# When weight slabs are requested in the last pass of an attention backward kernel, and which buffers the last ones use

## The chip, the cores and the metric

The kernel runs on one core of one Trainium2 chip. The metric is the time of one execution in device microseconds (us), the median of several runs. A profile is one further execution, recorded instruction by instruction. Engines are named as in the profile: PE (TensorE matmul) and PEld (its weight loads), DVE (VectorE), ACT (ScalarE), POOL (GpSimd), SP (SyncE). SP issues all loads of this kernel, POOL all its stores.

## The reference, cut to what matters

Two blocks alternate, twice each: an attention block for one token (1024 wide, 32 query heads, 4 groups of keys and values of 65,536 positions by 128) and a feed-forward block (3584 wide, squared ReLU). Both uses of a block share their weights and the K and V caches. The kernel returns the output and the gradients of everything for a given grad_out.

```
x = x + A(layernorm(x), K, V, wq, wo)
x = x + B(layernorm(x), w1, b1, w2, b2)
x = x + A(layernorm(x), K, V, wq, wo)
x = x + B(layernorm(x), w1, b1, w2, b2)
out, vjp = jax.vjp(f, x, K, V, wq, wo, w1, b1, w2, b2);  grads = vjp(grad_out)
```

The gradients of K and V are as large as the caches: 64 MB each in bf16 are read in every pass and, in the last one, written too.

## The kernel before, in words

The kernel goes over K and V four times: two forward passes (layers L1 and L3), a backward pass for L3 (`attn_bwd3`), and a last pass (`attn_bwd4`) that does the backward of L1 and writes the gradients of K and V for both layers. Between the passes stand dense stages for the feed-forward blocks. The change touches the last pass, which begins some 1,190 us into the execution.

**Items.** The last pass has 256 items, 64 for each of the 4 groups, in the order of groups 3, 2, 1, 0. An item is 8 columns of 128 positions. `pipeline` (line 828) counts iterations `i` (kept in `NOW["i"]`); a stage with lag n works on an item n iterations after its start. V is read up to 16 items ahead of the rest. Stages that matter here: `vT` (line 1316) turns V on PE (line 1324); `dV8` and `dK8` multiply out gradient blocks (`outer16`, PE line 1396), copy them from PSUM to the arena with ACT or DVE (`evac`, lines 161 and 164) and store them from POOL (line 1402); `k8` (line 1415) multiplies K blocks into the gradient of q (8 matmuls an item, line 1427). A K or V block of 1 MB serves 4 items. The forward passes and `attn_bwd3` run in an order written out by hand (`manual_schedule`); the last pass has none: there the instructions of each engine are put in order by a scheduler, with the program order as priority.

**Slots.** One SBUF tile, the arena, is cut into 20 slots of 1 MB (12 plus 8 that hold softmax numerators, given back as groups end). `take_one` (line 284) hands out a slot in program order, `give_slot` (line 319) takes it back. In the last pass the slots are split in two: a ring for stores (`RING`, 5 slots, and 2 more with each finished group), from which `fill=True` takes the oldest, and the other slots for loads, from which `fill=False` takes the oldest. A slot that was given back after a store counts as free 5 steps later (`STORE_STEPS`). The load itself can go out as soon as the slot's last user is done on the chip.

**Slabs.** `slabs` (line 433) yields a weight matrix row block by row block: in the last pass a slab is 4 row blocks, 1 MB, in one slot, requested by `fetch` at line 450. With `ahead=1` the next slab is requested only when the one before is used up.

**Row dots.** `g_rowdots` (line 565) multiplies 8 row blocks (two slabs) with a vector that is broadcast to all partitions (`g_bcast_vec`, line 547: a PE transpose, a small copy, 8 matmuls at line 558, two ACT copies to `vbc` at line 560). Each row block is one DVE product (line 586) and one ACT sum (line 575). It is a generator that `Background.step` (line 774) advances once an item; a yielded "wait" lets other background work go on in that item. In the last pass six of these jobs run, alternating wo (`g_dO`, for the next group) and wq (`g_dn`, for the group just ended): from iterations 32, 88, 119, 152, 183 and 218. Background work also holds `g_outer_wide` (line 1518), which keeps one load slot for long, and `g_outer`.

**The end.** 20 iterations before the end, two slabs of wq for the last group are requested (line 1845), 10 before the end `fill4` (line 1837) makes a `Rows` with two slots for turned parts (line 609) and fills them; `on4` (line 1818) finishes with the last group.

Of the kernel before, what the change touches and what calls it, by code (L numbers as in the profile page):

```python
# [20 lines left out]
def kernel(  # L21
# [31 lines left out]
    R = HQ // G  # L53
    F = B_w1.shape[1]
    DC, FC = D // P, F // P
# [10 lines left out]
    TLEAD = 2  # L66
    STORE_STEPS = 5
    WAIT_STEPS = 5
    NSLOT = 12
    NWT = 6  # L70
    NKEEP = [8, 7, 7]
# [10 lines left out]
    PS = {}  # L82
# [57 lines left out]
    load = {"act": 0.0, "dve": 0.0, "pe": 0.0}  # L140
# [289 lines left out]
    def f_rows_of(W):  # L430
        return W.rearrange("(s p j) n -> p s j n", p=P, j=4)

    def slabs(name, load, nk, kper, ncols, ahead=1, flat=False):
        pend = deque()
        ks = deque(range(0, nk, kper))

        def fetch():
            k = ks.popleft()
            i = None
            if ks and flat and NOW["wide"] and not odd_one():  # L440
                i = take_pair()
            if i is None:
                kn = min(kper, nk - k)
                sl = Slot(name)
            else:
                kn = min(2 * kper, nk - k)
                ks.popleft()
                sl = Slot(name, at=i, both=True)
            v = sl.t[:, 0:kn * ncols].rearrange("p (k n) -> p k n", n=ncols)
            nc.sync.dma_start(out=v, in_=load(k, kn))  # L450
            pend.append((k, kn, sl, v))

        def gen():
            while ks or pend:
                while ks and len(pend) < ahead:
                    fetch()
                k, kn, sl, v = pend.popleft()
                for kk in range(kn):
                    NOW["slab"] = sl
                    yield k + kk, v[:, kk, :]  # L460
                sl.over = True
                if not sl.users:
                    sl.free()
        g = gen()
        g_fetch = [fetch for _ in range(ahead)]
        return g, g_fetch
# [5 lines left out]
            f()  # L472
        return g

    def wq_slabs(g, ahead=1):
        v = rows_of(A_wq)
        return slabs("s_wq", lambda k, kn: v[:, k:k + kn, g * 1024:(g + 1) * 1024], DC, 4, 1024, ahead, True)

    def wo_slabs(g, ahead=1):
        v = rows_of(A_wo)  # L480
# [2 lines left out]
    def wo_runs(g):  # L483

        v = A_wo[g * 1024:(g + 1) * 1024, :].rearrange("(p k) n -> p k n", k=8)
        return slabs("s_wo", lambda k, kn: v[:, k:k + kn, :], R, 4, 1024, 1, True)[0]

    def w1_slabs(ahead=1):
        v = rows_of(B_w1)
# [72 lines left out]
            yield  # L562
        return vbc

    def g_rowdots(slab_it, nk, vcol, nj, finish, name):
        n = nj * P
        y = vec.tile([P, nk], F32, name=name)
        nc.gpsimd.memset(y[:], 0.0)
        vbc = None
        due = None  # L570
        steps = 8 if PS["pass4"] else WAIT_STEPS

        def total(t, kc):
            def f():
                nc.scalar.activation(out=t[:, :], in_=t[:, :], func=ACTF.Copy, accum_out=y[:, kc:kc + 1])  # L575
            return f
        for kc, slab in slab_it:
            if vbc is None:
                vbc = yield from g_bcast_vec(vcol, nj)
                for _ in range(steps - WAIT_STEPS + 1):  # L580
                    yield "wait"
            elif kc % 4 == 0:
                for _ in range(steps):
                    yield "wait"
            t = mvs.tile([P, n], BF, name="mv_t", tag="mv_t", bufs=2)
            nc.vector.tensor_tensor(out=t[:, :], in0=slab, in1=vbc[:, :], op=ALU.mult)  # L586
            add_load(dve=0.1 + n * 0.00054, act=0.42 + n * 0.00083)
            if due is not None:
                due()
            due = total(t, kc)  # L590
            yield
        due()
        yield
        r = finish(y[:, :])
        if r is not None:
            yield from r
        yield


    class Rows:  # L600
        def __init__(self, pool=None, bufs=NWT):
            self.pool, self.bufs = pool, bufs
            self.views = deque()
            self.n = 0
            self.parts = 0
            if pool is None:

                for _ in range(2):
                    t = Slot("s_wt").t[:, :].rearrange("p (v a b) -> p v a b", v=4, a=8)
                    self.views.extend(t[:, v, :, :] for v in range(4))  # L610
                self.bufs = 8
            self.queue = deque()
            self.jobs = deque()
            self.feed = None
# [282 lines left out]
    def gsl(g):  # L897
        return slice(g * R, (g + 1) * R)
# [10 lines left out]
    def g_wo(L, xacc, g, ps=ps_bg, it=None):  # L909
# [18 lines left out]
        orunb = tmp.tile([P, 8], BF, name="run_ob")  # L928
        nc.vector.tensor_copy(out=orunb[:], in_=oruns[:])
        yield  # L930
        yield from g_mv(wo_runs(g), R, 8, lambda kc: orunb[:, kc:kc + 1], ps, fin)


    def dO_finish(L, g):
# [43 lines left out]
        return fin  # L978

    def g_dn(L, dn, g, first):  # L980
        yield from g_rowdots(wq_slabs(g)[0], DC, L["dqT"][:, gsl(g)], R, dn_finish(dn, first), "%s_dn%d" % (L["name"], g))


    ACT_KT = (3, 13, 15)
# [607 lines left out]
    def pre_load(key, pair):  # L1592
        def f():
            PRE[key] = prefetch(pair())
        return f
# [241 lines left out]
    def fill4():  # L1837
# [4 lines left out]
        PRE["gwq"] = g_outer_last(bgpool, out_4, [L3["n"], L1["n"]], [L3["dqT"][:, gsl(lastg[3])], L1["dqT"][:, gsl(lastg[3])]],  # L1842
                                  lastg[3] * 1024)
        next(PRE["gwq"])
    attn_bwd4(3, L1, L3, on4, bg, b4, [(12 + B4_LAG, last_v), (20, pre_load("wq4", lambda: wq_slabs(lastg[3], 2))), (10, fill4)])
    b4.close()
    ps4_stack.close()

# [29 lines left out]
```

## Time and profile before

| what | value |
|---|---|
| median of 3 runs | 1952.98 us (1948.67 to 1953.23) |
| the profiled execution's own time | 1956.67 us |
| its span, first to last instruction | 1954.7 us |
| busy share of the span: PE, DVE, ACT, POOL | 82%, 60%, 53%, 7% |
| bytes moved | 787.64 MB, mean 403 GB/s |
| issue to landing, median: K and V blocks of 1 MB, slabs of wq in the last pass, stores of 1 MB | 15.6 and 13.1, 22.9, 16.5 us |

The page cuts the span into 40 slices of 48.9 us; a digit is a busy share in tenths, "DMA" the mean busy share of the 16 DMA engines, "GB/s" what they moved. A window view gives the same for any stretch. A waits view names who stood idle for whom: microseconds in total, how many times, and the longest. "issue" as a releaser means that the profile shows nothing that the engine waited for; a line of the engine's sequencer (DVEq) then shows the semaphore instruction that held it. Semaphore and DMA-issuing instructions do not count as busy. The median of K, V and store landings is that of the last pass.

### The profile page before, as it was taken

Reading aid. Unit: us, or ns where it says so; the run is one execution under the profiler, and the core shown is the slowest. Engines: PE = TensorE matmul, PEld = TensorE weight load, DVE = VectorE, ACT = ScalarE, POOL = GpSimd, SP = SyncE. Lnnn points to the kernel's source line nnn. Section 1 sums busy time; section 2 is a strip of 40 time slices with the busy share of each in tenths; the row PEclk is TensorE's granted clock in tenths of the full one; section 3 lists DMA queues with packets and bytes.
Section 4 is the critical chain, followed back from the end, with each engine's and each line's share of the span. In section 5 each row is a group of like instructions: output and inputs, shape, how many; then the busy total and the mean of one; then the engine's idle time right before and its main releaser. Section 6 shows DMA issues by size and latency. Waiting matters only on the chain. (4 is left out here: it accounts for less than half of the span.)

```text
span 1954.7 us, 67155 instructions
## 1 busy us (share of the span) xinstructions
PE 1598.7 (82%) x30319; PEld 1312.0 (67%) x30319; DVE 1167.6 (60%) x2421; ACT 1038.3 (53%) x1600; POOL 141.2 (7%) x321
## 2 busy tenths in 40 slices
PE   6878788687888878887787898888996987687977
PEld 6878778687777778777777785555554554454644
DVE  5655455255455544544454476867776886676866
ACT  3444334254334444435363465766876785576765
POOL 0000000000000000000000001111111211121211
PEclk9989899699899999898998999888888998897997
DMA  9999999999999998899999987999999999899997
GB/s 395 426 426 425 428 428 410 401 399 425 429 425 428 428 412 307 317 427 423 426 426 418 403 321 297 411 404 423 423 424 405 420 423 423 341 423 384 424 422 317
DMA packets 105997, 787.64 MB, mean 403 GB/s; under 512 B 9312, under 2 KB 16494, under 8 KB 42094
## 3 DMA queue, kind: packets, MB, share of 16 engines
q1 hardware_dynamic: 81630, 617.65, 76.6%
q0 software_dynamic: 24080, 165.70, 20.4%
q8 instruction: 237, 3.88, 0.7%
q14 instruction: 50, 0.41, 0.1%
HBM read 617.62 MB, written 165.69 MB: 401 GB/s over the span
## 5 line engine op out<-in xcount | busy, mean ns | idle before, releaser
L164 DVE COPY kt<-ps_tr 128x1024 bf16<-128x1024 bf16 x724 | 496.6, 688 | 439.5 <-PE ps_tr L1012 246.6
L161 ACT CAST arena<-ps_gg 128x1024 bf16<-128x1024 f32 x457 | 444.3, 1011 | 190.9 <-PE ps_gg L1396 147.0
L1012 PE MATMUL ps_tr<-ident_b,arena 128*128 128x128 bf16 x3840 | 309.0, 226 | 39.1 <-DMA arena<-in_A_k_cache_dram 26.6
L161 ACT COPY kt<-ps_tr 128x1024 bf16<-128x1024 bf16 x164 | 171.8, 1053 | 187.1 <-PE ps_tr L1204 118.1
L164 DVE CAST arena<-ps_gg 128x1024 bf16<-128x1024 f32 (+2 forms) x186 | 222.3, 1195 | 79.9 <-PE ps_gg L1396 35.0
L1012 PEld LDWEIGHTS <-arena 128*128 128x128 bf16 x3840 | 232.8, 101 | 47.9 <-DMA arena<-in_A_k_cache_dram 29.4
L1114 PE MATMUL ps_acc<-arena 128*128 128x64 bf16 (+4 forms) x4096 | 205.8, 196 | 61.5 <-DMA arena<-in_A_v_cache_dram 49.3
L1396 PE MATMUL ps_gg<-GG,xt 64*128 64x512 bf16 x1024 | 212.2, 412 | 47.5 <-DVE arena L164 35.0
L1114 PEld LDWEIGHTS <-arena 128*128 128x128 bf16 x4096 | 159.8, 101 | 66.3 <-DMA arena<-in_A_v_cache_dram 53.0
L1324 PE MATMUL ps_tr<-ident_b,arena 128*128 128x128 bf16 x1824 | 177.8, 233 | 30.3 <-DMA arena<-in_A_v_cache_dram 28.4
L1095 ACT ACTIVATE arena<-S_sb,L_negm 128x128 bf16<-128x128 f32 x256 | 165.6, 1003 | 66.0 <-DVE L_negm L1080 65.9
L1030 PE MATMUL ps_sc<-L_qpad,kt 128*128 128x64 bf16 (+7 forms) x3584 | 183.4, 195 | 15.0 <-ACT kt L161 7.1
L1204 PE MATMUL ps_tr<-ident_b,arena 128*128 128x128 bf16 x1920 | 157.1, 228 | 45.0 <-DMA arena<-in_A_v_cache_dram 43.4
L1324 PEld LDWEIGHTS <-arena 128*128 128x128 bf16 x1824 | 117.1, 103 | 86.1 <-issue 52.9
L1030 PEld LDWEIGHTS <-kt 128*128 128x128 bf16 x3584 | 153.3, 100 | 19.4 <-ACT kt L161 9.8
L1204 PEld LDWEIGHTS <-arena 128*128 128x128 bf16 x1920 | 119.2, 102 | 48.9 <-DMA arena<-in_A_v_cache_dram 46.7
L1427 PEld LDWEIGHTS <-arena 128*128 128x128 bf16 x2048 | 93.8, 102 | 62.9 <-issue 41.7
L1095 ACT ACTIVATION_READ_ACCUMULATOR arena<-S_sb,L_negm 128x1 f32 x256 | 128.0, 500 | 0.0
L1396 PEld LDWEIGHTS <-xt 64*128 64x128 bf16 x1024 | 65.1, 94 | 93.6 <-issue 54.7
L575 ACT ACTIVATE mv_t<-mv_t 128x1024 bf16<-128x1024 bf16 x96 | 102.0, 1064 | 41.7 <-DVE mv_t L586 41.6
L1355 PE MATMUL ps_sc<-DOB,kt 128*128 128x64 bf16 (+3 forms) x1824 | 113.6, 199 | 0.0
L1427 PE MATMUL ps_acc<-X,arena 128*128 128x64 bf16 (+3 forms) x1536 | 100.1, 198 | 14.9 <-DMA arena<-in_A_k_cache_dram 14.9
(306 smaller groups left out, 2161.4 us busy)
## 6 DMA issues: line engine op xcount, KB each, us to landing
arena<-in_A_k_cache_dram SPq DMA_DIRECT2D x86, 2048.0 KB, 21.5
arena<-in_A_v_cache_dram SPq DMA_DIRECT2D x83, 2048.0 KB, 21.0
out_dram<-arena POOLq DMA_DIRECT2D x149, 1024.0 KB, 16.5
arena<-in_A_v_cache_dram SPq DMA_DIRECT2D x76, 1024.0 KB, 14.2
arena<-in_A_k_cache_dram SPq DMA_DIRECT2D x76, 1024.0 KB, 15.1
arena<-in_A_wo_dram SPq DMA_DIRECT2D x22, 1024.0 KB, 14.0
arena<-in_B_w_dram SPq DMA_DIRECT2D x21, 1024.0 KB, 7.9
arena<-in_A_wq_dram SPq DMA_DIRECT2D x18, 1024.0 KB, 13.9
```

The lines of the kernel that those rows point to most:

```text
L161: nc.scalar.copy(out=out, in_=in_)
L164: nc.vector.tensor_copy(out=out, in_=in_)
L575: nc.scalar.activation(out=t[:, :], in_=t[:, :], func=ACTF.Copy, accum_out=y[:, kc:kc + 1])
L1012: nc.tensor.transpose(pt[:, i, :], kb8[:, i, :], ident_b[:, :])
L1030: nc.tensor.matmul(state["ps_s"][:, s:s + w, :].rearrange("p a b -> p (a b)"), lhsT=kt[:, i, :], rhs=L["qpad"][:, g, 0:w, :].rearrange("p ...
L1095: nc.scalar.activation(out=E(p, g, c0, SU)[:, :, h], in_=S[:, h, :], func=ACTF.Exp, bias=L["negm"][:, g, su, h:h + 1], scale=SCALE, accum_ ...
L1114: nc.tensor.matmul(ps_o[:, 0:w, :], lhsT=vb8[:, i, :], rhs=E(p, g, c, w), start=(c % SU == 0), stop=(c % SU == SU - 1), skip_group_check=True)
L1204: nc.tensor.transpose(pt[:, i, :], vb8[:, i, :], ident_b[:, :])
L1324: nc.tensor.transpose(pt[:, i, :], vb8[:, i, :], ident_b[:, :])
L1355: nc.tensor.matmul(state["ps_dp"][:, s:s + w, :].rearrange("p a b -> p (a b)"), lhsT=vt[:, i, :], rhs=DOB[:, g, 0:w, :].rearrange("p a b - ...
L1396: nc.tensor.matmul(pg[:, 512 * h:512 * h + 512], lhsT=xt[64 * h:64 * h + 64, j1 // 8 + m, :], rhs=gg[64 * h:64 * h + 64, :, :].rearrange(" ...
L1427: nc.tensor.matmul(ps_dq[:, 0:w, :].rearrange("p a b -> p (a b)"), lhsT=kb8[:, i, :], rhs=X[:, s:s + w, :].rearrange("p a b -> p (a b)"), ...
```

## The change

Three edits, all in the last pass:

- `g_rowdots` gets the slab generator together with its `fetch`. In the last pass it requests the first slab at once, lets 7 items pass, requests the second, then broadcasts the vector, and yields "wait" until 14 items have passed since a slab's request before it uses that slab. Both slabs are then held together for a while. In the other pass that uses it, the order stays as it was.
- The last two wq slabs take their slots from the ring of store slots (`fill=True`).
- The two slots for turned parts of `Rows` take theirs from the ring too.

```
+    LAND_STEPS = 14
...
-    def slabs(name, load, nk, kper, ncols, ahead=1, flat=False):
+    def slabs(name, load, nk, kper, ncols, ahead=1, flat=False, fill=False):
...
-                sl = Slot(name)
+                sl = Slot(name, fill)
...
-    def wq_slabs(g, ahead=1):
+    def wq_slabs(g, ahead=1, fill=False):
...
-    def g_rowdots(slab_it, nk, vcol, nj, finish, name):
+    def g_rowdots(pair, nk, vcol, nj, finish, name):
+        slab_it, (fetch,) = pair
...
-        steps = 8 if PS["pass4"] else WAIT_STEPS
+        due_at = deque()
+        if PS["pass4"]:
+
+            for h in range(2):
+                fetch()
+                due_at.append(NOW["i"] + LAND_STEPS)
+                for _ in range(LAND_STEPS // 2 if h == 0 else 0):
+                    yield "wait"
...
                 vbc = yield from g_bcast_vec(vcol, nj)
-                for _ in range(steps - WAIT_STEPS + 1):
+                if not PS["pass4"]:
                     yield "wait"
-            elif kc % 4 == 0:
-                for _ in range(steps):
+            elif kc % 4 == 0 and not PS["pass4"]:
+                for _ in range(WAIT_STEPS):
+                    yield "wait"
+            if PS["pass4"] and kc % 4 == 0:
+                for _ in range(due_at.popleft() - NOW["i"]):
                     yield "wait"
...
-                    t = Slot("s_wt").t[:, :].rearrange("p (v a b) -> p v a b", v=4, a=8)
+                    t = Slot("s_wt", True).t[:, :].rearrange("p (v a b) -> p v a b", v=4, a=8)
...
-    attn_bwd4(3, L1, L3, on4, bg, b4, [(12 + B4_LAG, last_v), (20, pre_load("wq4", lambda: wq_slabs(lastg[3], 2))), (10, fill4)])
+    attn_bwd4(3, L1, L3, on4, bg, b4, [(12 + B4_LAG, last_v), (20, pre_load("wq4", lambda: wq_slabs(lastg[3], 2, True))), (10, fill4)])
```

The remaining lines of the diff pass `fill` through and hand `wo_runs` and `wq_slabs` on as pairs.

## The prediction on record

> **What bounds the kernel now.** I read the page's slices first, then the stages of the last pass, then who waited for whom in it, then the groups of the disputed line.
>
> ```profile
> span 1954.7 us, 67155 instructions
> ...
> DMA  9999999999999998899999987999999999899997
> GB/s 395 426 426 425 428 428 410 401 399 425 429 425 428 428 412 307 317 427 423 426 426 418 403 321 297 411 404 423 423 424 405 420 423 423 341 423 384 424 422 317
> ```
>
> A slice is 48.9 us; the last pass begins in slice 24. Nearly every slice stands at 420 to 429 GB/s with the DMA engines full, so DMA bounds the kernel, and what can be gained is time in which DMA is not full: after slice 27 mainly slices 30, 34, 36 and 39. The chain of waits covers only the last 31 us and tells nothing of these. The stages:
>
> ```profile
> core 0: us, PE busy (x) PEld busy (x) DVE busy (x) ACT busy (x) POOL busy (x), PEclk, DMA share, GB/s
> ...
> 1500.00:1520.00 20.00, 17.38 (x213) 11.41 (x213) 14.58 (x29) 13.28 (x18) 3.07 (x6) 0.79 0.93 368
> 1600.00:1670.00 70.00, 55.72 (x756) 36.00 (x754) 51.38 (x97) 48.14 (x59) 11.06 (x21) 0.90 1.01 423
> 1675.00:1680.00 5.00, 0.00 (x0) 0.00 (x0) 0.00 (x0) 0.00 (x0) 0.00 (x0) 0.91 1.02 429
> 1680.00:1705.00 25.00, 16.52 (x197) 10.66 (x197) 15.53 (x27) 14.19 (x19) 3.23 (x7) 0.68 0.72 280
> ...
> 1790.00:1805.00 15.00, 12.15 (x135) 7.74 (x135) 11.84 (x19) 11.35 (x15) 2.51 (x5) 0.71 0.81 294
> 1805.00:1905.00 100.00, 85.34 (x1176) 54.42 (x1173) 75.32 (x145) 71.36 (x79) 20.87 (x37) 0.96 1.01 423
> 1905.00:1950.00 45.00, 38.79 (x460) 23.22 (x460) 29.77 (x54) 27.21 (x29) 7.56 (x12) 0.77 0.86 344
> ```
>
> At 1675 no engine works at all and DMA still runs at 429 GB/s; only after 1680 does it run dry. So a stop of the engines costs nothing until the transfers in flight are done. What stops them (waits of 1660 to 1690, then line 586 over the last pass):
>
> ```profile
> DVE mv_t L586 <- issue: 14.0, 1, 14.0
> ...
> PE ps_gg L1396 <- DVE arena L164: 13.1, 1, 13.1
> ```
>
> ```profile
> L586 DVE TENSOR_TENSOR mv_t<-arena,vbc x48: 669/682/912, 1233.9 to 1803.8; 128x1024 bf16<-128x1024 bf16 x48
> L586 DVEq EVENT_SEMAPHORE  x12: 21/50/14462, 1233.5 to 1779.0; - x12
> ...
>   issue: 29.4, 3
>   DMA arena<-in_A_wq_dram: 10.2, 1
> ```
>
> The product of line 586 needs its slab, vbc and mv_t. Each of the four long waits stands at the fifth product of a group, when vbc has served four products, so it is the second slab that is late. DVE stands, its evacuations stand behind the product, and PE waits for these: 10.2 us from 1485.8, 3.9 from 1585, 14.0 from 1672, 11.6 from 1779, in all 39.6 us.
>
> Why is it late? Eight weight loads of line 1427 are one item, so they date the items: 1668.4 us is item 191, 1778.7 item 227; an item takes 2.65 us between 231 (1799.8) and 263 (1884.5), 2.85 between 95 and 119. In the code the second slab of the job begun at item 183 is asked for at item 195 and used 8 items later. The trace has its request at 1666.8 and its first product's wait at 1672: outside the hand-ordered passes the program order is only a preference. A load goes out when its slot's last reader is done (by the slot lists, 5 items before 195), a product as soon as vbc is there. So the lead was 5 items less 3: 5.4 us instead of eight items. The same count gives 8 us for the job of item 218 (1771.3 to 1779.3) and 20.3 us for that of 119 (1465.5 to 1485.8). Slabs of wq land after
>
> ```profile
> DMA to landing us min/median/max: 19.5/22.9/26.3
> ```
>
> and by the waits' ends after 19.3, 19.5 and 30.5 us. All three leads are too short.
>
> **The change, part by part.** *Second slab.* No instruction is added or lost in the six jobs: the same 12 slab loads (0.33 to 0.90 us of SP each), 48 products (682 ns), 48 ACT sums (1070 + 203 ns). The request of the second slab moves from item i0+12 to i0+7. The broadcast (one transpose, a small copy, eight matmuls, two ACT copies of 0.58 to 0.63 us) moves from i0 to i0+7, which holds the first product to i0+11 at the earliest and the fifth to i0+15, however early the scheduler likes to place them. The lead becomes 8 items plus the age of the slot (5 to 8 items, by following the lists take_one and give_slot with the new request times): 13 to 16 items, at 2.65 us 34 to 42 us, over the longest landing seen, 30.5. The four waits should go. What they are worth is DMA time, not 39.6 us: against 424 GB/s, 20 x (1 - 368/424) = 2.6 us, 25 x (1 - 280/424) = 8.5 and 15 x (1 - 294/424) = 4.6, together 15.7 us; the 3.9 us wait left no dip. Bounds: 0 to -15.7. I take -13, since DMA after each dip also waits for engines that restart together.
>
> *A rule that bears on this.* While no engine worked, DMA moved 429 GB/s (stage 1675 to 1680). The Trainium skill, DMA: Bandwidth & Descriptors, section Issuing engines are not separate DMA queues, says that transfers issued by different engines interleave on the same 16 DMA engines; by it an earlier request takes its bandwidth from the K, V and store transfers beside it, and the 39.6 us of engine waits are no measure of the gain, as the row shows too. The same page, section Where 436 GB/s comes from, puts transfers between HBM and SBUF at about 358 GB/s; against that the dips would be worth 5.4 + 2.7 = 8.1 us, but 423 GB/s over 100 us is measured here and the measurement decides.
>
> *One load slot fewer.* Both slabs are held together from i0+7 to i0+18, where one was. Load slots are 7 in this stage; K and V hold two. By the lists, the loads with only 5 items (13 us) between the release of their slot and their use go from 10 to 23 after item 60, in items 160 to 175, 191 to 207 and 227 to 239, where the wide outer product holds a slot too. K and V land after medians of 15.6 and 13.1 us, so these become late next. What that costs is not shown directly. Below: 0, since the 10.8 us wait for V at 1628 stands in a stage with 423 GB/s. Above: as much as the late slabs cost, 15.7, if DMA runs dry as it did for them. It is nearer to the first row: behind a late K or V stand three to five further loads already asked for, behind the slab of 1666.8 only two. I take +2.
>
> *The end.* The last two wq slabs and the two buffers for turned parts come out of the ring of store slots, which has 11 by then. Now the K loads of the last items wait for slots:
>
> ```profile
> 1872.35 2.07 SPq L450 DMA_DIRECT2D arena<-in_A_wq_dram  x2
> 1882.93 37.09 SPq L353 DMA_DIRECT2D arena<-in_A_k_cache_dram  x4
> ```
>
> ```profile
> PE ps_acc L1427 <- DMA arena<-in_A_k_cache_dram: 10.7, 1, 10.7
> ```
>
> Four K loads go out between 1882.9 and 1919.7, the last two 34 us after the second; PE waits 10.7 us for the first at 1894, and the chain of waits starts where the third lands, at 1923.9. With four slots back, their slots are free 9 to 16 items ahead instead of 5 to 8, and all four go out by about item 263 (1884.5). The engines save up to 10.7 us, but the stores still have to drain: from 1905 to 1950 DMA loses 45 x (1 - 344/424) = 8.5 us, the most that can come back. At least 0: SP may stand before a ring slot whose store has not landed (median 16.5 us), with K and V loads queued behind it; by the lists these stores are 12 to 14 items (32 us or more) old, less the items by which SP runs ahead. The cover for that is the full DMA queue at 1805 to 1905; without it, up to 16.5 us. I take -4.
>
> *Sum.* -13 + 2 - 4 = -15 us. The profiled execution took 1956.67 us for a span of 1954.7, 3.7 us over the median 1952.98 of the runs; the same 15 us off the median gives **1938 us**. Its own bounds: -15.7 - 8.5 = -24 (1929) and about -7 (1946).
>
> **Rivals.** *Hidden again by K and V.* The slab waits go, but the loads with 5 items of lead run DMA dry in turn. For it: a dip of the same depth at 1290 to 1295, 259 GB/s, with a late K of 1.8 us near it. Against it: the V wait at 1628 without a dip. One dip of 5 x (1 - 259/424) = 1.9 us for each of the 13 newly short loads would be 25 us; about half of them eat most of the 17 us: 1953 - 3 = 1950 us.
>
> *Slower: the starved queue.* In the three stretches with 5 items of lead the engines stop for K or V as they stopped for slabs, and DMA runs dry each time by the 8.5 us of the worst slab stop, at both ends of each stretch: 6 x 5 = 30 us at a mean of 5, less the 17 saved, 13 us slower: 1966 us. It decides from the point at which these stretches lose more than 17 us of DMA. For it: landings of 20 us and more against 13. Against it: the loads queued behind.
>
> *It does not hold.* Waits in the program did not hold the products back before. Were the broadcast placed early as well, the fifth product would come at about i0+9, and the lead would be 7 to 10 items, 19 to 27 us against landings of 19 to 30: half of the slab gain, 1945 us. It counts inside the forecast's chance.
>
> **How the numbers follow.** A measurement can tell 0.3% (5.9 us) from no change: faster is under 1947.1, slower over 1958.9. Forecast with the third rival, 0.70, all faster; hidden again, 0.18, the same; starved, 0.12, slower. The range takes the forecast's bounds, a little under them for a fuller recovery of the end, and reaches up over the hidden case: 1927 to 1953.
>
> **What would show it.** Right: no wait over 4 us before line 586 after 1200; no engine-free stretch near 1490, 1675, 1785; slices 34 and 36 over 415 GB/s; the request of each second slab 30 us or more before its fifth product; the last K loads out before 1890 and no 10 us wait of line 1427. Wrong: line 586 still waits (third rival); or waits of lines 1324 and 1427 for K and V sum to more than before and dips stand in items 160 to 239 (first two); or SP stands for a store at the last wq slabs.

## The result, and the profile after

The changed kernel takes 1968.74 us (median of 6 runs, 1967.34 to 1970.04); the kernel before 1953.11 us (6 runs, 1948.67 to 1961.83). The ratio, of the means, is 1.0077, with a 95% interval of 1.0055 to 1.0099: **0.77% slower, some 15 us, where 15 us less were forecast.** The profiled execution took 1970.04 us, its span 1968.0. A tenth of a per cent is 2 us in what follows.

The slices of the page of the changed kernel, on the same scale as those of before:

```profile
span 1968.0 us, 67166 instructions
...
DMA  9999999999999998899999987999999999899995
GB/s 393 426 427 425 427 429 406 395 405 426 428 426 427 428 410 285 348 425 428 423 426 420 393 314 296 418 424 399 424 423 412 425 417 399 353 424 369 419 422 244
```

Slices 34 and 36, which were to rise over 415 GB/s, stand at 353 and 369 (before: 341 and 384). The last slice fell from 317 to 244. So the dips did not go, and the end became longer.

The product of line 598 (586 before), by the view of that line over the last pass:

```profile
L598 DVE TENSOR_TENSOR mv_t<-arena,vbc x48: 669/682/812, 1254.8 to 1828.2; 128x1024 bf16<-128x1024 bf16 x48
L598 DVEq EVENT_SEMAPHORE  x12: 21/50/50, 1253.2 to 1816.2; - x12
its engine sat idle before it (us, times) until:
  ACT vbc L561: 0.5, 1
```

The four waits for a second slab are gone: the longest semaphore instruction fell from 14462 to 50 ns. In their place PE stops for K and V. The waits from 1650 to 1672 us:

```profile
PE ps_acc L1439 <- DMA arena<-in_A_k_cache_dram: 8.2, 1, 8.2
...
PE ps_tr L1336 <- DMA arena<-in_A_v_cache_dram: 3.5, 1, 3.5
```

A pair like it stands at 1755 (7.2 us for K, 3.4 for V). Over the last pass (1190 us to the end) PE's waits for V and K sum to 47.9 us in the kernel before and to 64.3 in the changed one, one of the signs that the prediction had named for being wrong:

```profile
PE ps_tr L1324 <- DMA arena<-in_A_v_cache_dram: 28.4, 12, 10.4
PE ps_acc L1427 <- DMA arena<-in_A_k_cache_dram: 19.5, 6, 10.7
```

```profile
PE ps_tr L1336 <- DMA arena<-in_A_v_cache_dram: 37.3, 17, 7.2
PE ps_acc L1439 <- DMA arena<-in_A_k_cache_dram: 27.0, 6, 8.2
```

The stages around the first stop, and the end:

```profile
core 0: us, PE busy (x) PEld busy (x) DVE busy (x) ACT busy (x) POOL busy (x), PEclk, DMA share, GB/s
...
1655.00:1663.00 8.00, 0.43 (x10) 0.31 (x10) 1.82 (x2) 0.45 (x1) 1.15 (x2) 0.74 1.01 422
1663.00:1685.00 22.00, 17.90 (x142) 9.31 (x142) 7.83 (x11) 9.69 (x10) 2.22 (x4) 0.50 0.68 266
1685.00:1700.00 15.00, 14.12 (x205) 10.06 (x204) 12.93 (x21) 11.19 (x15) 2.83 (x6) 0.96 0.95 348
...
1920.00:1950.00 30.00, 27.98 (x378) 18.10 (x375) 21.41 (x46) 20.93 (x25) 3.65 (x6) 0.86 0.59 242
```

As before, DMA is full during the stop (422 GB/s) and runs dry after it, with TensorE at a granted clock of 0.50. Against 423 GB/s, 22 us at 266 and 15 at 348 lose 22 x (1 - 266/423) + 15 x (1 - 348/423) = 8.2 + 2.7 = 10.9 us, more than the worst slab stop had cost (8.5). From 1920 to 1950 PE is busy for 28 of 30 us while DMA moves 242 GB/s: there the engines bind.

Why the load comes late, from SP's queue:

```profile
1654.04 0.38 SPq L451 DMA_DIRECT2D arena<-in_A_wq_dram  x1
1655.23 0.33 SPq L354 DMA_DIRECT2D arena<-in_A_v_cache_dram  x1
1681.34 0.33 SPq L354 DMA_DIRECT2D arena<-in_A_k_cache_dram  x1
1682.86 0.33 SPq L354 DMA_DIRECT2D arena<-in_A_v_cache_dram  x1
```

After the second slab's request of 1654.0 one V load goes out and then none for 26 us. The trace's slab requests and products show how long slabs are held: in the changed kernel 39 to 68 us lie between the request of a slab and its first product (13 to 60 us before). Where the trace has the landing, a slab of wq landed after 20.8 to 32.4 us and one of wo after 8.4. The two load slots are occupied and unused for much of that.

That explains this stop, but not yet the time. The kernel before has a gap of 24 us behind its slab of 1666.8, and experiment e9 below, which is level with the kernel before, has both the gap of the changed kernel and its stop (waits for V and K of 63.6 us in all). Before (the row merges two K loads, one at its start and one at its end), and then e9 with its stage after the stop:

```profile
1668.57 24.21 SPq L353 DMA_DIRECT2D arena<-in_A_k_cache_dram  x2
```

```profile
1654.74 0.33 SPq L354 DMA_DIRECT2D arena<-in_A_v_cache_dram  x1
1680.19 0.33 SPq L354 DMA_DIRECT2D arena<-in_A_k_cache_dram  x1
```

```profile
1663.00:1685.00 22.00, 18.20 (x146) 9.50 (x147) 8.24 (x12) 9.40 (x10) 2.21 (x4) 0.50 0.82 320
```

### The profile page after: what moved, and what is told of

It reads as the page before. It is cut to its first block, busy times and chain, and to the rows that moved or that the text cites. A ratio compares the mean times of both kernels' runs of the same rounds, so it can differ in the third digit from the quotient of the medians.

```text
span 1968.0 us, 67166 instructions
## 1 busy us (share of the span) xinstructions
PE 1610.6 (82%) x30319; PEld 1310.8 (67%) x30319; DVE 1171.3 (60%) x2421; ACT 1038.3 (53%) x1600; POOL 144.3 (7%) x321
## 5 line engine op out<-in xcount | busy, mean ns | idle before, releaser
L162 ACT CAST arena<-ps_gg 128x1024 bf16<-128x1024 f32 (+2 forms) x457 | 445.0, 1007 | 236.0 <-PE ps_gg L1408 153.8
L165 DVE CAST arena<-ps_gg 128x1024 bf16<-128x1024 f32 (+1 forms) x186 | 223.3, 1201 | 115.8 <-PE ps_gg L1486 59.3
L1408 PE MATMUL ps_gg<-GG,xt 64*128 64x512 bf16 x1024 | 216.5, 424 | 19.1 <-ACT arena L162 7.6
L1042 PE MATMUL ps_sc<-L_qpad,kt 128*128 128x64 bf16 (+7 forms) x3584 | 182.3, 194 | 15.3 <-ACT kt L162 8.8
L1042 PEld LDWEIGHTS <-kt 128*128 128x128 bf16 x3584 | 151.5, 100 | 20.3 <-ACT kt L162 12.0
L1216 PEld LDWEIGHTS <-arena 128*128 128x128 bf16 x1920 | 117.6, 101 | 47.9 <-DMA arena<-in_A_v_cache_dram 44.8
L1367 PEld LDWEIGHTS <-kt 128*128 128x128 bf16 x1824 | 85.4, 103 | 41.0 <-issue 39.9
L1261 PE MATMUL ps_acc<-dsT,arena 128*128 128x64 bf16 (+7 forms) x2048 | 102.2, 194 | 8.5 <-DMA arena<-in_A_k_cache_dram 6.2
## 6 DMA issues: line engine op xcount, KB each, us to landing
arena<-in_A_k_cache_dram SPq DMA_DIRECT2D x76, 1024.0 KB, 15.3
```

Source lines behind the costliest of these rows:

```text
L162: nc.scalar.copy(out=out, in_=in_)
L165: nc.vector.tensor_copy(out=out, in_=in_)
L1042: nc.tensor.matmul(state["ps_s"][:, s:s + w, :].rearrange("p a b -> p (a b)"), lhsT=kt[:, i, :], rhs=L["qpad"][:, g, 0:w, :].rearrange("p ...
L1216: nc.tensor.transpose(pt[:, i, :], vb8[:, i, :], ident_b[:, :])
L1261: nc.tensor.matmul(ps_dq[:, 0:w, :].rearrange("p a b -> p (a b)"), lhsT=kb8[:, i, :], rhs=dsT[:, s:s + w, :].rearrange("p a b -> p (a b)") ...
L1367: nc.tensor.matmul(state["ps_dp"][:, s:s + w, :].rearrange("p a b -> p (a b)"), lhsT=vt[:, i, :], rhs=DOB[:, g, 0:w, :].rearrange("p a b - ...
```

## The experiments

All kernels compute the whole reference. Ratios are to the kernel before, run on the same chip beside them, with 95% intervals; its medians in these sets are 1955.6 to 1957.2 us, against 1953.11 beside the changed kernel, which was run in that first set alone. "Background steps left" is counted by following the code: the steps of outer products that the last pass has not done when it drains its background work at iteration 273. It is 1 in the kernel before and 4 in the changed one; a step is mostly a 128 x 1024 block, 256 KB of output.

**Which edit is it?** Two theories: the end part costs about 10 us (A), or the row dots cost it all (B). *e1, row dots alone:*

```
-                    t = Slot("s_wt", True).t...
+                    t = Slot("s_wt").t...
-    ... pre_load("wq4", lambda: wq_slabs(lastg[3], 2, True)) ...
+    ... pre_load("wq4", lambda: wq_slabs(lastg[3], 2)) ...
```

> The changed kernel with the end as before: the last two wq slabs and the two buffers for turned parts come from load slots again; the six row-dot jobs request their slabs early, as in the change. Theory A (the row dots swap one stop for another of the same price, the end part costs the rest): 1955 to 1959 us, no wait of over 4 us at the product's line, DMA dips near items 191 to 207 and 227 to 235, an end like before's. Theory B (the two held slabs starve K and V, and that is the whole loss): 1965 to 1970 us.

Measured 1970.1 us, ratio 1.006 [1.0038, 1.0082]. *e2, the end alone:* the kernel before, with the last two wq slabs and the two `s_wt` slots from the store ring.

```
-                    t = Slot("s_wt").t...
+                    t = Slot("s_wt", True).t...
-    ... pre_load("wq4", lambda: wq_slabs(lastg[3], 2)) ...
+    ... pre_load("wq4", lambda: wq_slabs(lastg[3], 2, True)) ...
```

> The kernel before with the end part of the change alone: the last two wq slabs and the two buffers for turned parts come from the ring of store slots; the row dots as before. Theory A: 1961 to 1965 us, with SP standing before a wq slab's ring slot near the end for 10 us or more and the last four K loads going out behind it. Theory B: 1949 to 1954 us.

Measured 1960.04 us, 1.0021 [1.0012, 1.0031]. Most of the loss belongs to the row dots: e1 lies where theory B had it, and e2 in neither range, under the 1961 to 1965 of A and over the 1949 to 1954 of B. The end part cost 4 us there instead of gaining 4.

**Is it the slab waits or the slot?** *e3* leaves the requests as they were and broadcasts the vector a second time before the second slab's products, so that these products can't come early; no second slot is held.

```
             elif kc % 4 == 0:
-                for _ in range(steps):
+                for _ in range(steps - 4 if PS["pass4"] else steps):
                     yield "wait"
+                if PS["pass4"]:
+                    vbc = yield from g_bcast_vec(vcol, nj)
```

> The kernel before, with one edit: in the six row-dot jobs of the last pass the vector is broadcast a second time ahead of the second slab's products (4 items of waiting and 4 of broadcast in place of 8 of waiting), so that these products cannot be placed before that broadcast. Slots and requests are as before: one slab at a time. It adds six times one transpose, eight matmuls and two ACT copies. Theory A and B alike (a slab that is late because its products come early is cured without a second slot): the waits over 4 us at the product's line go, K and V keep their leads, and up to the 15.7 us of DMA dips come back: 1938 to 1948 us. If engine stops only move on to the next load whatever the leads are: 1950 to 1955 us.

Measured 1996.33 us, 1.0213 [1.019, 1.0236]. Far out of any expectation. The count explained where to look: the second broadcast's four steps take the place of waits in which background work ran, and 22 background steps are left for the end. *e5* is e3 with these four steps yielded as "wait", so that the other work goes on beside them (1 step left):

```
-                    vbc = yield from g_bcast_vec(vcol, nj)
+                    again = g_bcast_vec(vcol, nj)
+                    while True:
+                        try:
+                            next(again)
...
+                        yield "wait"
```

> As the second broadcast, but its four steps are yielded as waiting steps, so that other background work goes on in the same items. Steps of background work left for the closing drain: 1, as before the change (22 with the plain second broadcast). Theory C (the 40 us of the plain second broadcast are work put off to the end, where it has no cover): 1950 to 1962 us, with the stretch from item 275 to the end near 25 us again instead of 49. Rival D (they come from K and V stops after the slab stops went, by way of the halved clock after each stop): 1980 us or more.

Measured 1963.86 us, 1.0037 [1.0021, 1.0052], 32 us under e3 and 2 us over the range of theory C: background work that is put off is a cost by itself. And the slab stops are gone in e5 (the longest semaphore instruction of its product line is 50 ns), while K and V keep their slots, without any gain. It carries six more broadcasts, whose own cost was not taken apart. Its waits from 1640 to 1680, and 1895 to 1915:

```profile
PE ps_tr L1333 <- DMA arena<-in_A_v_cache_dram: 6.4, 1, 6.4
```

```profile
PE ps_acc L1436 <- DMA arena<-in_A_k_cache_dram: 12.9, 1, 12.9
```

*e4* is e1 with the slabs of the row-dot jobs taken from the store ring as soon as it has more than 6 slots, so that K and V keep theirs:

```
-                sl = Slot(name, fill)
+                sl = Slot(name, fill or (PS["pass4"] and ahead == 1 and len(RING) > 6))
```

> As the row dots alone, but in the last pass the slabs of these jobs come from the ring of store slots once it has more than six (five of the six jobs), so that K and V keep their load slots. Theory B: the K and V stops at items 160 to 240 go, 10 us or more faster than the row dots alone. Theory A: the stops at K and V go too, but SP stands before ring slots whose stores have not landed, with K and V loads behind it: within 5 us of the row dots alone, or slower.

Measured 1960.13 us, 1.0031 [1.0015, 1.0048], against 1.006 for e1: 10 us less by the medians, as theory B had it, but 0.29% or 6 us by the ratios, which is barely more than the two intervals allow. In the bad stretch, e1 and then e4 (e1's profiled execution, 1960.49 us, was the fastest of its five; the other four took 1967.85 to 1971.37):

```profile
1663.00:1685.00 22.00, 18.20 (x164) 9.86 (x163) 9.56 (x13) 10.18 (x11) 2.21 (x4) 0.58 0.67 258
```

```profile
1663.00:1685.00 22.00, 18.62 (x160) 10.22 (x160) 9.72 (x13) 9.64 (x11) 2.21 (x4) 0.53 0.86 331
```

*e8* asks for the price of a load slot in the kernel before: `NRING = 6` gives the store ring one slot more and the loads one less, all through the pass.

```
-    NRING = 5
+    NRING = 6
```

> The kernel before with one slot moved from loads to stores (ring of 6 instead of 5) for the whole last pass; row dots and end as before. The slot lists give loads of K and V a mean of 6.3 items between release and use, against 8.1 before and 7.5 with the change (44 loads of 102 at 5 items or less, against 8 and 24). If the short leads are what the early requests cost (12 us for 0.6 items): 25 to 40 us slower than before. If they cost nothing while DMA is full: within 5 us of before.

Measured 1980.89 us, 1.0127 [1.0107, 1.0147]: 24 us for one load slot, a little under the 25 to 40 that short leads were to cost.

**What does put-off background work cost?** *e6* is e4 with `bg.steps` lowered, so that the background work of the pass is due 20 items before the last instead of 4 (1 step left); *e7* is the kernel before with the same edit (0 left).

```
-    bg.steps = len(ITEMS[3]) - 4
+    bg.steps = len(ITEMS[3]) - 20
```

> The slabs from the ring, with background work paced to be done 16 items earlier: 1 step left for the drain instead of 4. Theory C: 3 steps at about 1.2 us each, 3 to 5 us faster than the slabs from the ring, 1954 to 1957 us beside a kernel before of 1956. Rival D: within 2 us of the slabs from the ring, since their end is set by a 13.5 us stop for K and the clock after it.

> The kernel before with the same pacing, as a control: no step left for the drain instead of 1. Theory C: within 3 us of before. Rival D: the same; if pacing by itself moves stops about, it shows here as more than 3 us.

Measured 1955.42 us, 0.9993 [0.998, 1.0005], for e6, and 1955.2 us, 0.999 [0.9976, 1.0003], for e7. Both came as theory C had them. Of all kernels with split requests e6 is the fastest, and it is no faster than the kernel before. In its profile the stretch of the loads is much mended: SP's last load before the gap goes out at 1659.7 and the next at 1676.9, and the windows are

```profile
1663.00:1685.00 22.00, 18.57 (x219) 10.81 (x217) 12.71 (x18) 12.83 (x14) 2.74 (x5) 0.78 0.99 387
1685.00:1700.00 15.00, 14.48 (x202) 9.53 (x199) 13.91 (x24) 14.27 (x20) 3.59 (x7) 1.00 1.01 423
```

*e9 to e12.* e9 is the changed kernel with the edit of e6; e10 the kernel before with `NRING = 4`, one load slot more; e11 is e9 with `NRING = 4`, e12 is e6 with it.

> The changed kernel whole, but the background work of the last pass is to be done 20 items before the last instead of 4, so that 1 step of it is left for the end instead of 4. The slots that K and V wait for hardly change (loads with 5 items of lead: 21 instead of 24). Theory of two prices: the loss of about 15 us against the kernel before is some 10 us for the second load slot held and 4 us for put-off work; only the second goes here, so the ratio to the kernel before falls from 1.0077 to about 1.005 to 1.006 (4 to 5 us under the changed kernel, as the same edit brought 4.7 us between the two kernels with slabs from store buffers). Rival, put-off work is nearly the whole loss: 1.000 to 1.002. Rival, it costs nothing in this kernel since stores bind the end: 1.0077.

> The kernel before with 4 store buffers in the ring at first instead of 5, and so one slot more for loads all through the last pass: by the slot lists the mean lead of K and V loads rises from 8.1 to 9.9 items, none under 6, and the second slabs of wq are asked for 8 to 9 items after their slot came free instead of 5 to 7. Theory that the leads of all loads (slabs, K, V) price the last pass: the four stops for second slabs shrink to one or none over 4 us, stops for V too, and it is 5 to 15 us faster than the kernel before, the mirror of the 24 us that one slot less cost, and smaller since a lead over some 9 items brings nothing. Rival, the store side is as tight as the load side: with 4 buffers the gradient copies wait for stores (median landing 16.5 us), ratio 1.002 to 1.01. Rival, DMA is full anyway and leads are enough: 0.998 to 1.001.

> The changed kernel with both prices given back: early background work as in the first kernel of this call, and one store buffer less in the ring, so that the K and V loads have one load slot more (mean lead 9.3 items, 14 of 102 under 8, none under 6). Theory of two prices: 10 us under the first kernel of this call and so about level with the kernel before or up to 10 us faster (0.995 to 1.001); and it is not faster than the kernel before with the same store buffer given up, by more than 3 us, if the slabs' waits cost little once their slots come earlier. Rival, the split request itself costs (its own waits and placing): it stays at 1.004 or more.

> The version of the earlier runs that was level with the kernel before (split slab requests in wo and wq jobs from store buffers, the end as before, background work early) with 4 store buffers at first instead of 5: K and V loads get a mean lead of 10.9 items, none under 6 and one under 9. If load leads are what the time goes by, it is the fastest of all, 5 to 12 us under the kernel before (0.994 to 0.997). Rival, the store ring, which now also holds the slabs, is too small: gradient copies wait for stores, some slabs get slots with stores only 2 to 4 items past their landing time, and SP, which must wait for these, holds K and V loads back: 1.002 or more.

Measured: e9 1957.83 us, 1.001 [0.9996, 1.0024]; e10 1956.14 us, 1.0002 [0.9989, 1.0016]; e11 1969.0 us, 1.0074 [1.0055, 1.0092]; e12 1965.37 us, 1.0054 [1.0035, 1.0073]. All four went against the theory that I favoured. e9 went to the rival: with nothing but its background work earlier, the changed kernel is within measurement of the kernel before. And a theory fell that I had formed after e4 and e8, that load leads price the whole pass: a mean lead of 9.9 items instead of 8.1 gains nothing (e10), and with split requests the smaller store ring costs 12 us (e9 to e11, e6 to e12). With split requests five store slots at first are better than four; the kernel before does as well with four. Which wait makes e11 and e12 slow was not followed further; e11's PE stops for 15.3 us at 1482 and 16.0 at 1900.

**The middle or the end?** Early background work moves two things: in e9 three steps more are done by iteration 118 already, and three fewer are left at 273. e13 changes only the end of the changed kernel, e14 only the end of e9, e16 only the end of the kernel before; e15 is e1 with early background work. e13:

```
                 else:
                     self.done += 1
-                    return
+                    if not (PS["pass4"] and NOW["i"] in (256, 259, 262)) or twice:
+                        return
+                    twice = True
```

e14 (on e9) and e16 (on the kernel before), in `Background.step`:

```
+            if PS["pass4"] and NOW["i"] in (267, 269, 271):
+                return
             while self.normal and self.done < self.total * i / self.steps:
```

> The changed kernel, and only late in its last pass three items (iterations 256, 259 and 262) do two background steps instead of one, so that 1 step is left for the closing drain instead of 4; everything up to iteration 256 is as in the changed kernel, its middle loss of DMA time with it. Theory that the loss is the put-off steps, by their place at the end: 7 to 12 us under the changed kernel, 1.001 to 1.004. Rival, the early background work gained by shifting the middle of the pass (DMA lost up to 1840 us fell from 22.4 to 14.3 us there): it stays at 1.006 to 1.008.

> The changed kernel with early background work (1.001), in which only iterations 267, 269 and 271 do no background step, so that 4 steps are left for the closing drain as in the changed kernel; its middle is that of the kernel with early background work. Theory that the put-off steps cost by their place at the end: 1.005 to 1.008. Rival, the middle of the pass gained: 1.001 to 1.003.

> The row dots part alone (1.006 before, with 4 steps left at the end) with early background work (1 step left); the end's buffers as in the kernel before. Theory of put-off steps: 0.997 to 1.001, as the whole change with early work was 1.001 and the end part alone 1.002. Rival, the second load slot held costs 10 us of itself, as the 10 us between this part with its slabs from load slots and from store buffers had it: 1.004 to 1.006.

> The kernel before, in which only iterations 267, 269 and 271 do no background step, so that 4 steps are left for the closing drain instead of 1, and nothing else of the change. Theory that three steps put off cost by their place at the end: 7 to 12 us, 1.004 to 1.006. Rival, they cost only where the end's stores already bind: under 3 us, 1.000 to 1.0015.

Measured: e13 1965.26 us, 1.0054 [1.0034, 1.0074]; e14 1957.91 us, 1.0019 [1.0004, 1.0033]; e15 1961.07 us, 1.0027 [1.0014, 1.0041]; e16 1957.58 us, 1.0013 [0.9999, 1.0027]. e14 and e16 went to the rival, e13 and e15 fell between the two. The end alone is worth 0.23% (changed kernel to e13), 0.09% (e9 to e14) and 0.13% (before to e16), 2 to 4.5 us each, and none of the three is clearly beyond its intervals; the larger part, 0.44% (e13 to e9) and 0.58% (changed kernel to e14), goes with where the background work stands in the middle.

*e17 and e18* test that part by itself. e17 is the kernel before, in which iterations 100, 101 and 102 do no background step (the skip of e16) and 256, 259 and 262 two (the edit of e13). e18 is the changed kernel, in which 100, 106 and 121 do two.

```
+            if PS["pass4"] and NOW["i"] in (100, 101, 102):
+                return
```

```
+                    if not (PS["pass4"] and NOW["i"] in (100, 106, 121)) or twice:
+                        return
+                    twice = True
```

> The kernel before, in which iterations 100, 101 and 102 do no background step and iterations 256, 259 and 262 do two, so that its background work is three steps behind from 102 to 262, where the change puts it, and 1 step is left for the end as before; row dots, slots and end are untouched. Theory that being behind is the price by itself: 5 to 10 us, 1.003 to 1.005. Rival, being behind costs only together with the second slab held (the row dots' 24 items of two slots fall on other parts of the wide outer product): 0.999 to 1.001.

> The changed kernel, in which iterations 100, 106 and 121 do two background steps, so that from there on its background work stands where the kernel before has it (74, 87, 107 steps done by 151, 183, 217 against 74, 86, 107) and 1 step is left for the end; nothing else is moved. Theory that the three steps put off, in the middle and at the end, are what the change loses: 1.000 to 1.003, as with the background work of the whole pass done early (1.001). Rival, the early pace helped by something else, over the whole pass: 1.005 to 1.008.

Measured: e17 1963.63 us, 1.0038 [1.0025, 1.005]; e18 1960.27 us, 1.0016 [1.0001, 1.003]. Both as the theory had it. Three background steps late from iteration 102 to 262 cost the kernel before 0.38%, with nothing of the change in it; and the same three steps given back take 0.61% off the changed kernel's 0.77%.

| kernel | slabs held in | steps done by 118, 217 | left at 273 | ratio |
|---|---|---|---|---|
| before | one load slot | 55, 107 | 1 | 1 |
| e17 | one load slot | 52, 104 | 1 | 1.0038 |
| e16 | one load slot | 55, 107 | 4 | 1.0013 |
| changed | two load slots | 53, 104 | 4 | 1.0077 |
| e13 | two load slots | 53, 104 | 1 | 1.0054 |
| e14 | two load slots | 56, 107 | 4 | 1.0019 |
| e9 | two load slots | 56, 107 | 1 | 1.001 |
| e18 | two load slots | 55, 107 | 1 | 1.0016 |
| e1 (end as before) | two load slots | 53, 104 | 4 | 1.006 |
| e15 (end as before) | two load slots | 56, 107 | 1 | 1.0027 |
| e4 (end as before) | store ring | 53, 104 | 4 | 1.0031 |
| e6 (end as before) | store ring | 56, 107 | 1 | 0.9993 |

## Why the prediction was wrong, point by point

**A term was missing: the background work that the moved waits displace.** Two steps of the prediction failed. Its largest term, -13 us for the second slab, came to 0 (next paragraph). And it took "No instruction is added or lost in the six jobs" for the whole cost of moving the jobs' waits. That count holds, but a "wait" of a job is the item in which other work goes on, and I put the moved waits at nothing without a reason. Seven of them now stand at a job's front, and where the background work is not behind its quota there (`self.done < self.total * i / self.steps`) it takes no step: in three of the seven in the job begun at iteration 88. By the code, in that job the kernel before does 12 background steps in the waits (92 to 95, 100 to 107), the changed one 10 (89, 90, 92, 94, 99 to 101, 106 to 108). After that one step or one job takes nearly every item, and nothing catches up: 53 steps instead of 55 by 118, 104 instead of 107 by 217, 4 left instead of 1. The runs price this at 12 to 13 us in the changed kernel (e18, e9), 6.5 in the row dots alone (e1 to e15), 7.5 with slabs in the ring (e4 to e6); in the kernel before 7 us for the middle (e17) and 2.5 for the end (e16). What stands at the end can be seen from 1930 us on. The casts of ACT and DVE that leave outer products and K and V gradients in the arena, before:

```profile
L161 ACT CAST arena<-ps_gg 128x1024 bf16<-128x1024 f32 x11 | 11.2, 1014 | 5.5 <-PE ps_gg L1474 4.1 <-PE ps_gg L1396 1.4
L164 DVE CAST arena<-ps_gg 128x1024 bf16<-128x1024 f32 x5 | 6.1, 1222 | 1.1 <-PE ps_gg L1396 0.5 <-PE ps_gg L1474 0.5
```

in the changed kernel:

```profile
L162 ACT CAST arena<-ps_gg 128x1024 bf16<-128x1024 f32 x17 | 17.0, 1014 | 9.6 <-PE ps_gg L1486 4.7 <-PE ps_gg L1408 3.8 <-ACT rowa L162 0.6
L165 DVE CAST arena<-ps_gg 128x1024 bf16<-128x1024 f32 x11 | 13.5, 1224 | 7.3 <-PE ps_gg L1486 4.1 <-PE ps_gg L1408 2.9
```

and in e9:

```profile
L162 ACT CAST arena<-ps_gg 128x1024 bf16<-128x1024 f32 x8 | 8.1, 1012 | 7.7 <-PE ps_gg L1486 6.8 <-PE ps_gg L1408 1.0
L165 DVE CAST arena<-ps_gg 128x1024 bf16<-128x1024 f32 x6 | 7.3, 1221 | 2.4 <-PE ps_gg L1408 1.3 <-PE ps_gg L1486 1.0
```

The columns are count, busy time and mean, then the idle time before. 28 casts lie in the changed kernel's closing stretch, 16 in that of before, 14 in e9's. Iteration 275 (by the weight loads of the K products) is reached at 1930.9 us in the changed kernel and at 1930.1 before, and the end comes 37.1 us later there against 24.6. But the 12 casts more are no count of the put-off steps: half of them belong to gradients of K and V (24 matmuls of line 1408 from 1930 us on, 12 of line 1396 before), e13 has 22 casts with 1 step left, and e16 has 16, as before, with 4. What the end costs by itself is told by e13, e14 and e16 alone, and barely.

**Second slab, -13 us: the waits went, the gain did not come.** That the mechanism holds is seen in the view of line 598, and the lead of the second slab became longer than I said: 44 to 61 us from its request to the fifth product, not 34 to 42. But e6, with the slabs in the ring and its background work in place, stands at 0.9993 beside 0.999 for the kernel before with the same early work (e7): the gain is 0, give or take some 3.5 us. e5 has no slab stops, the slots of before, six more broadcasts, and 1.0037. The engines run on to the next thing that DMA is late with, K or V, and DMA runs dry after that stop as it did after the old one. That is the mechanism of my rival "hidden again by K and V". Loss against 423 GB/s from 1500 to 1840, from windows of 160, 60 and 120 us: before 2.3 + 9.4 + 4.5 = 16.2, e6 1.1 + 1.7 + 7.7 = 10.5, e9 3.8 + 6.4 + 2.8 = 13.0 us, the changed kernel 1.9 + 10.8 + 6.8 = 19.5. One profile can't be read finer: e9 and e14, one program up to iteration 266, have 13.0 and 18.7 (their profiled executions took 1957.14 and 1964.46 us).

**One load slot fewer, +2 us: mis-sized.** From e1 to e4 and from e15 to e6, where only the slots of the slabs differ, it is 0.29% and 0.34%: 6 to 7 us. In the whole change it may be less: e9 and e18 leave 2 to 3 us for all but the put-off work. My count of loads with 5 items of lead was near (24 against 23 by the lists of the changed kernel), but I priced them by the V wait at 1628, behind which the loads go on. The 26 us without a load behind the slab of 1654.0 are the case that I had put aside under "behind a late K or V stand three to five further loads already asked for"; but e9 has that gap too, so by itself it is not what the change lost.

**The end, -4 us: not shown, and more likely a loss where work is put off.** Alone it cost 4 us (e2). With early background work the whole change stands 0.17% below the row dots alone (e9, e15), without it 0.17% above (changed, e1); neither difference is beyond the intervals. I had named the price, SP before a ring slot:

```profile
1882.72 4.97 SPq L451 DMA_DIRECT2D arena<-in_A_wq_dram  x2
1887.79 6.48 SPq L354 DMA_DIRECT2D arena<-in_A_k_cache_dram  x4
```

In the changed kernel the two slabs go out at 1882.7 and 1887.3 (before: 1872.3 and 1874.0), and four K loads stand behind them. These do go out together, by 1894 as against 1920 before, and the wait for K fell from 10.7 to 7.5 us; but from 1920 on the engines bind, and earlier loads gain nothing there. In e9, whose ring slots come free earlier, the slabs go out at once:

```profile
1872.81 0.38 SPq L451 DMA_DIRECT2D arena<-in_A_wq_dram  x1
...
1875.76 0.38 SPq L451 DMA_DIRECT2D arena<-in_A_wq_dram  x1
```

**The rivals.** "Starved queue" gave 1966 us with 0.12 and stands nearest to the time, and the stops for K and V and the dips behind them are what it spoke of; but that is in good part luck: the slot accounts for 6 to 7 us of the loss at most, e9 has such a stop without the loss, and most of the rest is a term that no rival had. "It does not hold" is refuted: the products were held. The sum as the runs have it, for the row dots: 0 for the slab waits, +6 to 7 for the slot, +6.5 to 7.5 for put-off work, together 13 against 12 measured (e1). For the whole change put-off work weighs 12 to 13 and what remains is 2 to 3 us; the two prices are not independent of each other and of the end part.

**What stays open.** Three steps are 0.75 MB at most, 1.8 us at 423 GB/s, and three or so evacuations of 1.0 to 1.2 us. Being late with them through the middle costs 7 us (e17), far more than they are. Through which wait was not found: the dips of e17 from 1500 to 1840 sum to 14.0 us, no more than those of the kernel before, and a single profile does not resolve it. One candidate that no run moved alone is the wide outer product, which keeps a load slot: by the code it gives the slot back in iteration 237 in e17 and in the changed kernel, in 234 in the kernel before, in 230 in e9 and e18. No kernel here beat the kernel before by more than its interval.

## What to carry to other kernels

When a job's waits are moved, ask what used them: list the work of lower priority that ran there, count it up to the places where it must be done, and price what is left for a stage in which other engines bind. Where DMA bounds a stage, an engine's stop is worth only what DMA loses after it; remove it and the engines wait for the next load, so a request that is made earlier than its landing needs (here 39 to 68 us for landings of 8 to 32) only takes a slot from that load. And before a cause is settled, put the suspected side effect alone into the old kernel and take it alone out of the new one: e17 and e18 said what the runs with larger edits had not.

## What the runs showed of the hardware

I had not reckoned with TensorE's clock after a stop. Two stages of the kernel before, from the end of its K stop of 10.7 us on, and one of the changed kernel behind its stop of 7.5:

```profile
1900.00:1910.00 10.00, 5.06 (x42) 2.75 (x43) 2.32 (x3) 2.02 (x2) 0.00 (x0) 0.50 1.01 424
1910.00:1920.00 10.00, 10.00 (x89) 5.74 (x86) 6.12 (x9) 4.63 (x5) 0.82 (x2) 0.50 0.86 332
```

```profile
1910.00:1920.00 10.00, 8.22 (x74) 4.71 (x75) 3.99 (x5) 3.40 (x4) 1.26 (x2) 0.50 1.01 427
```

After every stop of PE of 3 us or more in the last pass of these two kernels the granted clock is 0.50, for 4 to 26 us from PE's restart on. It also falls where no stop was longer than 2 us, and PE's work does not soon bring it back: a stage of the kernel before that begins so, and the changed kernel behind its stop of 1655, both with PE busy throughout (by the profile, which models the ends of matmuls and may hide short gaps):

```profile
1280.00:1293.00 13.00, 13.00 (x104) 6.88 (x102) 7.55 (x17) 6.30 (x7) 1.62 (x3) 0.50 0.93 389
```

```profile
1670.00:1685.00 15.00, 15.00 (x124) 8.03 (x122) 7.83 (x11) 8.19 (x9) 2.22 (x4) 0.50 0.54 199
```

It is in this phase, not in the stop, that DMA ran dry (266 GB/s from 1663 to 1685; 46 GB/s from 1670 to 1675). That the clock makes the dip was not tried. It does not make one by itself: from 1910 to 1920 the changed kernel has 0.50 and 427 GB/s; and the gap in the loads stands at the place of the dip.

The Trainium skill, TensorE: Matmul & The Clock Gate, section Part 1: The HAM clock gate, says that an idle window of about 3.4 us throttles the array to half its clock and that about 3.4 us of sustained work release it. The first half agrees with the long stops here, though the clock fell after shorter ones too; the second does not, where the clock stayed at half through 13 and 15 us with PE busy throughout.
